# Attention, a feed-forward layer and a soft mixture of experts in one kernel: logits of the last token block taken four neuron groups at a time, its slot chain in column halves, the third block split earlier

## The chip, the core and the metric

The kernel runs on one core of one Trainium2 chip. The metric is the device time in microseconds (us) of one execution; a lower time is better. Engines are named as the profile names them: PE (TensorE), PEld (its weight loads), DVE (VectorE), ACT (ScalarE), POOL (GpSimd), SP (SyncE, which here issues every DMA).

## The reference, cut to what matters

Three stages follow each other. The constants are 4 batches, 8 heads, 576 positions, 2304 tokens, width 512, 2048 hidden neurons, 8 experts with 4 slots each (32 slots), 1024 expert neurons.

```python
def _moe_ref(x, w_in, w_out):                 # after block-causal attention; x is [2304, 512]
    h = x @ w_in                              # [2304, 2048]
    g = np.where(h >= 1, h, np.where(h <= -1, 0.0, (h + 1) ** 2 / 4))
    return (g @ w_out).astype(np.float32)

def _moe2_ref(x, phi, w1, w2):
    logits = x @ phi                          # [2304, 32]
    d = softmax over tokens (axis 0) of logits
    slot_input = (d.T @ x).reshape(8, 4, 512)
    for e in range(8):
        h = np.maximum(slot_input[e] @ w1[e], 0.0)      # w1[e] is [512, 1024]
        slot_out[e] = h @ w2[e]                         # w2[e] is [1024, 512]
    c = softmax over slots (axis 1) of logits
    return c @ slot_out                       # [2304, 512]
```

## The kernel before, in words

**Attention** (lines 46 to 345) fills the first 202 us. It leaves x transposed in SBUF: for token blocks 0 and 1 already split into a high and a low float32r part (`xt`), for blocks 2, 3 and 4 as float32 (`xw`).

**The main loop** is in `run` (L868). `BLK` (L322) has five token blocks: four of 512 tokens, the last (block 4) of 256. `UNITS` lists 69 units (b, f): token block b times one of 16 groups f of 128 hidden neurons. `h_unit` (L537) computes one unit with 12 matmuls `h`: four slices of the width times three products of high and low parts (L535). `act_unit` then makes the neurons' values `g` on ACT, POOL and DVE. Units 0 to 20 treat blocks 0 and 1 alternately and need the weight tiles `w7` to `w15`, which are still being made: a raw double `raw` is loaded, ACT scales it (`w_mul`, L457), DVE takes bits apart (`w_bits`, L463 to L466), ACT casts (L254), POOL subtracts and adds (`w_parts`, L481, L482). From unit 18 on the same is done for 16 tiles of `w_out`, where POOL adds (L474), SP stores the sum to DRAM, and PE transposes it (`wo_turn`, L495) and multiplies it by phi (`wo_phi`, L504, `wo_back`, L513) into `w2p`, which is w_out times phi. So the logits of a block are g times `w2p`.

`split(2)` (L402) takes block 2 apart: ACT casts 128x1024 values to the high part `xh` (L408), POOL subtracts to get the low part `xl` (L409), for each of two halves `u`. It stands at units 18 and 19, three units ahead of the block's first unit.

Side steps hang on unit numbers in `plan_sides` (L813): `put(k, step)` runs a step after unit k, on every engine's queue in that order. For a block they are, for each quarter q of the neuron groups and each pair u of 128-token tiles: `half` (L580; PE transposes g into `gn`, L592, ACT copies it out), with the fourth-group logits at the last u (`logits`, L599: matmuls `lt` with 32 output rows, at row 0, 32, 64 or 96 of one PSUM bank, L604); then `soft` (softmax over tokens with a running maximum), `disp` (transposes the exponentials, `et`), `slots` (L637: exponentials times `gn`, matmuls `s`, L642; DVE adds them to the running sums S, L650), and `weigh` (softmax over slots). In block 4 each of the four output places of `lt` takes the same 256 tokens (L603), so the four places hold equal copies. After block 3 `maximum`, `weights` and `total` fold the four places of S into the one tile `T`.

**The chain** (L913): `last` (the last transposes and the last four groups' logits), `soft4`, `disp4`, `slots4` (L751), two `turn` (transposes, L765), `inputs` (L768: matmuls `si` with w_out tiles `wo`, L775, which give the slots' inputs), `spread` (L779: `t_i`, and copies into `st`). **The tail** (L986) multiplies by the experts' weights: `w1` (matmuls `eh`, L998), transposes `et` of the hidden values `hN`, `w2` (matmuls `acc`, L1025), then the outputs (L1044 to L1084). The combine weights are transposed by `comb` (L973) from `n4`, made by `comb_parts` (L961): twice in the chain, three times in the tail.

**The experts' weights** come in 72 pieces `ew`: 32 of w1 (512 KB each), 24 of the first 340 columns of w2 (`in_w2a_dram`), 16 of the other 172 (`in_w2b_dram`). They go into the slots of two SBUF pools with 27 and 22 slots, which g, gn, x, w and the rest use as well. `feed` (L929) runs after each unit from 30 on and after each step of the chain and the tail; it issues up to four pieces if `room` (L351), which looks ahead on a recorded plan of slot use, leaves `spare` = 3 slots free (0 from the chain on). SP issues strictly in this order, and each DMA waits until its slot's last reader is done and until the DMA eight before it has landed.

Of the kernel before, what the change touches and what calls it, by code (L numbers as in the profile page):

```python
# [11 lines left out]
ALU = mybir.AluOpType  # L12
# [304 lines left out]
class Moe:  # L317
# [5 lines left out]
    ASIDE = 2  # L323
    CAP = {"b4": 27, "c4": 22}
# [30 lines left out]
    def room(self, key):  # L355
# [143 lines left out]
    def wo_phi(self, c):  # L499
# [7 lines left out]
        wp = self.wp = e.sp.tile([P, P], F32, tag="wp", bufs=1, name=f"wp{c}")  # L507
# [72 lines left out]
    def half(self, b, q, u):  # L580
# [5 lines left out]
        if u == 0 and q == 0 and b != 1:  # L586
            self.lt[b] = e.ppv.tile([P, 512], F32, tag="pv", name=f"lt{b}")
# [5 lines left out]
        if u == n // 256 - 1:  # L593
            self.logits(b, fs)
# [4 lines left out]
    def logits(self, b, fs):  # L599
        nc, lt = self.nc, self.lt[b]  # L600
        for f in fs:
            for j in range(4):
                o, n = (0, 256) if b == 4 else (j * P, P)  # L603
                nc.tensor.matmul(lt[32 * j:32 * j + 32, 0:n], self.e.w2p[:, f], self.gt(b, f)[:, o:o + n],  # L604
                                 start=(f == 0), stop=(f == 15))


    def soft(self, b):
# [3 lines left out]
        v["lts"] = sp.tile([P, P], F32, tag="lts", bufs=1, name=f"lts{b}")  # L612
        E = v["E"] = sp.tile([P, P], F32, tag="E", bufs=1, name=f"E{b}")
# [16 lines left out]
    def disp(self, b):  # L630
# [3 lines left out]
        v["en"] = e.sp.tile([P, P], F32, tag="en", bufs=1, name=f"en{b}")  # L634
# [17 lines left out]
    def weigh(self, b):  # L652
# [6 lines left out]
        else:  # L659
            for j in range(2):  # L660
                nc.tensor.transpose(ps[:, 32 * j:32 * j + 32], self.EL[0:32, 1, j * P:(j + 1) * P], e.ident[0:32, 0:32])
# [14 lines left out]
    def maximum(self):  # L676
# [5 lines left out]
        row = self.row = sp.tile([1, 4, 32], F32, tag="row", bufs=1, name="row")  # L682
# [28 lines left out]
    def last(self):  # L711
# [8 lines left out]
        self.logits(4, range(12, 16))  # L720
# [4 lines left out]
    def soft4(self):  # L725
        e, nc, sp = self.e, self.nc, self.e.sp
        lt = self.lt[4][:, 0:256]
        EL = self.EL
# [4 lines left out]
        nc.scalar.activation(EL[0:32, 0], lt[0:32], AF.Exp, bias=nm[0:32], accum_out=l[0:32])  # L733
# [482 lines left out]
```

## Time and profile before

| | us |
|---|---|
| median of three runs (lowest to highest) | 530.07 (528.93 to 530.76) |
| the profiled execution, its run time | 532.08 |
| its span in the profile | 530.2 |
| PE busy | 506.9 (96%) |
| PEld, DVE, ACT, POOL busy | 386.1, 335.5, 324.4, 202.0 |
| DMA | 91.01 MB, mean 172 GB/s |

The run time is the span and 1.9 us around it. The profile says for each engine when it was busy, for idle time what ended it, and for the whole program a chain of work followed back from the last instruction. Busy shares are averages over stages that have different limits; the stages here are attention (to 202), the main loop (to 466), the chain (to 479) and the tail.

### The profile page before, as it was taken

What the parts mean: (1) busy time and instruction counts of PE and PEld (TensorE: products, weight loads), DVE (VectorE), ACT (ScalarE), POOL (GpSimd) and SP (SyncE); (2) the same over time, 40 slices, a digit from 0 to 9 for tenths busy, and PEclk for the clock granted to TensorE, in tenths of its full rate; (3) what the DMA queues carried; (4) which work ended last, traced back from release to release, by engine and by line L of the source; (5) the groups of instructions that cost most, each with busy time, mean ns of one, the idle gap of its engine ahead of it and who ended that gap; (6) DMA issues with size and microseconds to landing.
All of it is one profiled execution on the core that took longest, in us unless ns stands there. A gap on an engine that the chain in (4) does not pass through costs nothing.

```text
span 530.2 us, 11838 instructions
## 1 busy us (share of the span) xinstructions
PE 506.9 (96%) x4538; PEld 386.1 (73%) x4538; DVE 335.5 (63%) x678; ACT 324.4 (61%) x732; POOL 202.0 (38%) x259
## 2 busy tenths in 40 slices
PE   6899999999999999999899999899999999989994
PEld 5688887888878787877677887788658888643463
DVE  6769988888887746888987646723554442521242
ACT  4879998888877634767868878633335444321131
POOL 3888997776777312554733214400001000000000
PEclk8779999999999999999999999999999999999998
DMA  6235435343311147113147773512266495899997
GB/s 200 91 81 163 126 84 150 90 122 101 85 53 28 51 138 285 43 40 99 56 167 230 284 268 110 178 42 80 96 255 215 131 405 172 312 329 383 410 413 297
DMA packets 42711, 91.01 MB, mean 172 GB/s; under 512 B 8736, under 2 KB 18080, under 8 KB 42656
## 3 DMA queue, kind: packets, MB, share of 16 engines
q1 hardware_dynamic: 42656, 90.26, 50.1%
q8 instruction: 36, 0.59, 0.5%
q14 instruction: 19, 0.16, 0.1%
HBM read 74.51 MB, written 14.68 MB: 168 GB/s over the span
## 4 chain that ended last, share of the span: by engine, by line
PE 82%; DVE 5%; DMA 4%; ACT 4%; issue 2%; POOL 1%; SPq 0%; ACTq 0%; DVEq 0%; POOLq 0%
PE h L535 32%; PE sc L120 7%; PE gn L592 5%; PE om L189 5%; PE lt L604 4%; PE s L642 3%; PE eh L998 3%; PE sc L113 3%; PE ps_1p L171 3%; PE ps_2p L171 2%; PE ps_3p L171 2%; PE ps_0p L171 2%; PE acc L1025 2%; PE om L194 2%; DVE wab L464 1%
## 5 line engine op out<-in xcount | busy, mean ns | idle before, releaser
L535 PE MATMUL h<-xh,w 128*128 128x512 f32 (+1 forms) x384 | 115.6, 369 | 0.0
L535 PE MATMUL h<-xt,w 128*128 128x512 f32 x384 | 99.4, 403 | 0.0
L163 POOL TENSOR_SCALAR pr<-pr,sm 128x512 f32<-128x512 f32 (+2 forms) x144 | 88.5, 632 | 25.3 <-DVE sm L158 23.6
L151 ACT ACTIVATE pr<-sc,nm 128x512 f32<-128x512 f32 (+2 forms) x144 | 78.2, 551 | 10.1 <-DVE nm L146 8.3
L569 DVE SCALAR_TENSOR_TENSOR g<-g 128x512 f32<-128x512 f32 (+1 forms) x52 | 36.9, 710 | 66.9 <-ACT g L556 66.3
L535 PEld LDWEIGHTS h<-xh,w 128*128 128x128 f32 x384 | 69.1, 189 | 13.7 <-issue 3.8
L535 PEld LDWEIGHTS h<-xt,w 128*128 128x128 f32 x384 | 68.3, 188 | 14.1 <-POOL w L482 1.8
L535 PE MATMUL h<-xl,w 128*128 128x512 f32 (+1 forms) x192 | 68.2, 355 | 0.3 <-POOL xl L409 0.3
L146 DVE TENSOR_REDUCE nm<-sc 128x2 f32<-128x1024 f32 (+1 forms) x64 | 52.3, 819 | 21.5 <-PE sc L126 21.1
L570 DVE TENSOR_TENSOR g<-h,g 128x512 f32<-128x512 f32 (+1 forms) x80 | 50.8, 636 | 15.7 <-ACT g L561 13.7
L556 ACT ACTIVATE g<-h,half 128x512 f32<-128x512 f32 (+1 forms) x52 | 32.3, 622 | 44.5 <-PE h L535 43.1
L673 POOL TENSOR_TENSOR cn<-cn,cm 128x128 f32<-128x128 f32 (+1 forms) x5 | 1.9, 379 | 140.7 <-DVE cm L672 140.7
L120 PE MATMUL sc<-K,Q 64*128 64x512 f32 (+3 forms) x384 | 47.6, 363 | 3.7 <-ACT pr L151 2.6
L254 ACT COPY gn<-gn 128x1024 f32<-128x1024 f32 x35 | 35.3, 1009 | 16.0 <-PE gn L592 15.9
L120 PEld LDWEIGHTS sc<-K,Q 64*128 64x128 f32 x384 | 30.2, 196 | 14.0 <-issue 6.1
L535 PEld LDWEIGHTS h<-xl,w 128*128 128x128 f32 x192 | 36.4, 189 | 4.5 <-POOL xl L409 0.7
L474 POOL TENSOR_TENSOR wab<-wab 128x512 f32<-128x512 f32 x16 | 22.0, 1374 | 40.4 <-DVE wab L466 20.5
L481 POOL TENSOR_TENSOR wab<-wab,w 128x256 f32<-128x256 f32 (+1 forms) x23 | 22.6, 982 | 37.5 <-ACT w L254 20.3
L592 PE MATMUL gn<-ident,g 128*128 128x128 f32 x280 | 36.5, 273 | 0.1
L592 PEld LDWEIGHTS gn<-ident,g 128*128 128x128 f32 x280 | 31.9, 140 | 5.2 <-issue 2.5
L464 DVE SCALAR_TENSOR_TENSOR wab<-wab 128x512 uint32<-128x512 uint32 (+1 forms) x39 | 28.5, 731 | 10.3 <-ACT wab L457 7.0
L558 ACT ACTIVATE g<-h,half 128x512 f32<-128x512 f32 x28 | 19.2, 686 | 22.2 <-PE h L535 20.0
(222 smaller groups left out, 898.1 us busy)
## 6 DMA issues: line engine op xcount, KB each, us to landing
ew<-in_w_dram SPq DMA_DIRECT2D x32, 512.0 KB, 5.6
raw<-in_w_in_dram SPq DMA_DIRECT2D x16, 512.0 KB, 5.8
raw<-in_w_out_dram SPq DMA_DIRECT2D x16, 512.0 KB, 4.2
ew<-in_w2a_dram SPq DMA_DIRECT2D x16, 510.0 KB, 9.1
ew<-in_w2b_dram SPq DMA_DIRECT2D x16, 344.0 KB, 6.7
kn<-in_k_dram SPq DMA_DIRECT2D x16, 288.0 KB, 3.2
qn<-in_q_dram SPq DMA_DIRECT2D x16, 288.0 KB, 4.4
vn<-in_v_dram SPq DMA_DIRECT2D x16, 256.0 KB, 3.4
```

The lines of the kernel that those rows point to most:

```text
L120: nc.tensor.matmul(sc[:, h, 0:n], self.Q[r, qa, 128 * i:128 * i + 128], self.K[r, ka, 0:n], start=(k == 0), stop=False)
L146: nc.vector.tensor_reduce(out=self.negm[:, 2 * i:2 * i + 2], in_=self.scs[i][:, :, 0:128 * (i + 1)], axis=AX.X, op=ALU.max, negate=True)
L151: self.nc.scalar.activation(pr, sc, AF.Exp, bias=self.negm[:, b:b + 1], accum_out=self.acc[:, b, 0:1])
L163: self.nc.gpsimd.tensor_scalar(out=pr, in0=pr, scalar1=self.sums[:, b:b + 1], scalar2=1.0, op0=ALU.mult, op1=ALU.mult)
L171: nc.tensor.transpose(ps[:, u * P:(u + 1) * P], self.pr[b][:, kc * P:(kc + 1) * P], e.ident)
L254: nc.scalar.copy(dst, src)
L464: v.scalar_tensor_tensor(out=Au, in0=Au, scalar=3, in1=Bu, op0=ALU.logical_shift_left, op1=ALU.bitwise_or)
L535: nc.tensor.matmul(ph[:, 0:n], w[:, wi, kk], self.x(b, kk, xi)[:, 0:n], start=(kk + m == 0), stop=(kk + m == 5))
L556: nc.scalar.activation(g, ph, AF.Relu, bias=e.half[:, 0:1], scale=0.5)
L569: nc.vector.scalar_tensor_tensor(out=g, in0=g, scalar=1.0, in1=g, op0=ALU.min, op1=ALU.mult)
L570: nc.vector.tensor_tensor(out=g, in0=ph, in1=g, op=ALU.max)
L592: nc.tensor.transpose(ps[:, j, i * P:(i + 1) * P], self.gt(b, f)[:, o:o + P], e.ident)
```

## The change

**Logits of block 4.** For groups f below `SPLIT` = 14 one matmul takes place of four: group f goes to output place f % 4 alone, in columns 256 to 511 of the bank, so that the four places hold partial sums of different groups. `gather` (after the third `half`) does groups 12 and 13 and lets ACT copy the partial sums to `part`; `collect` adds the four places with one 128x256 matmul by `sel4` into columns 0 to 255. Groups 14 and 15 are added there as before, by four matmuls each.

**Order.** Block 3's logits are all computed right after block 2's `soft`, in two batches of eight groups, and no longer between block 3's transposes; `soft`, `disp`, `slots`, `maximum`, `weights`, `weigh` and `total` of blocks 2 and 3 move up, block 3's first `slots` by five units. `split(2)` is called before unit 0 and at unit 1 in place of units 18 and 19. The POOL subtraction of every `split` is done in two halves of 128x512.

**Chain.** `slots4`, `inputs` and `spread` are done by column halves u = 0, 1, each with a PSUM tile of its own, and `spread(1)` stands inside the first `w1` group. `comb` for blocks 2 and 3 moves from the tail into the chain, and `comb` works on 64 columns where it had the same 64 twice (ACT copies the result twice).

**Slots.** The tiles `EL`, `E`, `en`, `lts` and `wp` become parts of one fixed tile `y`, which frees one slot from unit 65 on. `room` leaves 3 slots free up to unit 57, then 1. SP's order of DMAs is the same in both kernels.

```diff
+    SPLIT = 14
...
-            if base + len(gone) - k > self.cap - (self.spare if t < self.bend else 0):
+            if base + len(gone) - k > self.cap - (3 if t < self.middle else 1 if t < self.bend else 0):
...
-                self.nc.gpsimd.tensor_tensor(out=lo, in0=self.xw[i, u], in1=hi.bitcast(F32), op=ALU.subtract)
+                for a in range(0, 1024 // n, 512 // n):
+                    c = slice(a, a + 512 // n)
+                    self.nc.gpsimd.tensor_tensor(out=lo[:, c], in0=self.xw[i, u][:, c], in1=hi[:, c].bitcast(F32), op=ALU.subtract)
...
     def logits(self, b, fs):
...
+            if b == 4 and f < self.SPLIT:
+                j = f % 4
+                nc.tensor.matmul(lt[32 * j:32 * j + 32, 256:512], self.e.w2p[:, f], self.gt(b, f),
+                                 start=(f < 4), stop=(f + 4 >= self.SPLIT))
+                continue
             for j in range(4):
                 o, n = (0, 256) if b == 4 else (j * P, P)
...
+    def gather(self):
+        self.logits(4, range(12, self.SPLIT))
+        self.part = self.e.sp.tile([P, 256], F32, tag="part", bufs=1, name="part")
+        self.nc.scalar.copy(self.part, self.lt[4][:, 256:512])
+
+    def collect(self):
+        self.nc.tensor.matmul(self.lt[4][:, 0:256], self.e.sel4, self.part, start=True, stop=False)
...
-        self.logits(4, range(12, 16))
+        self.collect()
+        self.logits(4, range(self.SPLIT, 16))
...
+    def slots4(self, u):
+        e, nc = self.e, self.nc
+        ps, o = e.psc.tile([P, 2, 512], F32, tag="sc", name=f"s4{u}")[:, 0, 0:256], slice(256 * u, 256 * u + 256)
         for j in range(2):
             for c in range(4):
-                nc.tensor.matmul(ps[32 * c:32 * c + 32], self.EL[:, 2, 32 * j:32 * j + 32], self.gn[4, c, 0][:, j],
+                nc.tensor.matmul(ps[32 * c:32 * c + 32], self.last_en[:, 32 * j:32 * j + 32], self.gn[4, c, 0][:, j, o],
                                  start=(j == 0), stop=(j == 1))
...
+        for u in range(2):
+            ps, o = self.si[u], slice(256 * u, 256 * u + 256)
+            for t in (2 * r, 2 * r + 1):
...
+            if r == 1:
+                e.copy("A", self.T[:, o], ps)
...
+            if b == 2:
+                put(free, "soft", 2)
+                for i, step in enumerate((("disp", 2), ("weigh", 2), ("logits", 3, range(8)))):
+                    put(free + 1, *step)
+                for i, step in enumerate((("slots", 2, 0), ("logits", 3, range(8, 16)), ("soft", 3))):
+                    put(free + 2, *step)
+                put(free + 3, "slots", 2, 1)
+                put(free + 4, "disp", 3)
+                put(free + 6, "maximum")
+                put(free + 7, "weights")
+                put(free + 8, "weigh", 3)
+        put(at_half[3, 1] + 2, "slots", 3, 0)
+        put(free + 1, "slots", 3, 1)
+        put(free + 2, "total")
...
+        self.w_mul(READY)
+        self.w_bits(READY)
+        parts = list(self.split(2))
+        parts[0]()
         for k, (b, f) in enumerate(units):
...
+            if k == 1:
+                parts[1]()
...
-        steps = (self.soft4, lambda: self.comb(0), self.disp4, lambda: self.comb(1), self.slots4, self.clear,
-                 lambda: self.turn(0), lambda: self.turn(1), lambda: self.inputs(0), lambda: self.inputs(1), self.spread)
+        steps = ((self.soft4,), (self.comb, 0), (self.comb, 1), (self.disp4,), (self.slots4, 0),
+                 (self.slots4, 1), (self.clear,), (self.turn, 0), (self.comb, 2), (self.turn, 1), (self.inputs, 0),
+                 (self.inputs, 1), (self.spread, 0), (self.comb, 3), (self.drop, "n4"))
...
-        w1(0)
+        w1(0, lambda: self.spread(1))
```

How the order moves, at three places. First POOL where the main loop begins: `pr` is attention's last work there, `wab` and `w` are `w_parts` of the weight tiles 7 and 8. Before:

```order
L163 TENSOR_SCALAR pr_184<-pr_184,sm_3_2763 128x128
L481 TENSOR_TENSOR wab_3046<-wab_3046,w_3070 128x512
L482 TENSOR_TENSOR w_3070<-wab_3046 128x512
L481 TENSOR_TENSOR wab_3090<-wab_3090,w_3119 128x512
L482 TENSOR_TENSOR w_3119<-wab_3090 128x512
```

Now:

```order
L163 TENSOR_SCALAR pr_184<-pr_184,sm_3_2763 128x128
L412 TENSOR_TENSOR xl_3054<-xw_148,xh_3053 128x512 x2
L484 TENSOR_TENSOR wab_3047<-wab_3047,w_3076 128x512
L485 TENSOR_TENSOR w_3076<-wab_3047 128x512
L412 TENSOR_TENSOR xl_3081<-xw_149,xh_3080 128x512 x2
L484 TENSOR_TENSOR wab_3101<-wab_3101,w_3130 128x512
L485 TENSOR_TENSOR w_3130<-wab_3101 128x512
```

Two halves of `xl` stand ahead of tile 7's pair, and two ahead of tile 8's.

Second PE at the last logits, in `last` and the chain's first steps; `gn` are the transposes, `ct` is `comb`, `et` is `disp4`. Before:

```order
L716 MATMUL gn_5670<-ident,g_12_5477 128x128 x6
L604 MATMUL lt_5434<-g_12_5477,w2p 32x256 x16
L716 MATMUL gn_5670<-ident,g_12_5477 128x128 x2
L973 MATMUL ct_5708<-identr,n_5526 128x128 x4
L743 MATMUL et_5715<-ident,EL 128x32 x2
L973 MATMUL ct_5719<-identr,n_5526 128x128 x4
```

Now:

```order
L733 MATMUL gn_5633<-ident,g_12_5516 128x128 x6
L622 MATMUL lt_5488<-part,sel_124 128x256
L613 MATMUL lt_5488<-g_12_5516,w2p 32x256 x8
L733 MATMUL gn_5633<-ident,g_12_5516 128x128 x2
L1004 MATMUL ct_5660<-identr,n_5565 64x128 x4
L1004 MATMUL ct_5668<-identr,n_5565 64x128 x4
L760 MATMUL et_5675<-ident,y 128x32 x2
```

Sixteen narrow matmuls became eight and one wide one, and both `ct` stand ahead of `et`.

Third PE at block 3's first `slots` (matmuls `s`). Before, they stand between units h_12 and h_13 of block 4, ahead of `t_m` (`maximum`):

```order
L642 MATMUL s_5481<-gn_5087,en_5432 32x512 x2
L642 MATMUL s_5481<-gn_5143,en_5432 32x512 x2
L642 MATMUL s_5481<-gn_5190,en_5432 32x512 x2
L642 MATMUL s_5481<-gn_5251,en_5432 32x512 x2
L681 MATMUL t_m<-ident,nm 1x128
```

Now, between h_7 and h_8:

```order
L593 MATMUL gn_5313<-ident,g_8_4575 128x128 x2
L593 MATMUL gn_5313<-ident,g_10_4645 128x128 x2
L658 MATMUL s_5324<-gn_5122,y 32x512 x2
L658 MATMUL s_5324<-gn_5202,y 32x512 x2
L658 MATMUL s_5324<-gn_5249,y 32x512 x2
L658 MATMUL s_5324<-gn_5287,y 32x512 x2
L538 MATMUL h_8_5342<-xh_4835,w_3130 128x256
```

The four `gn` tiles that `s` reads last become free for pieces `ew` five units sooner.

## Rows read from the trace of the kernel before

**Rows 1.** The page: busy time, share of the span and instructions

```profile
PE 506.9 (96%) x4538; PEld 386.1 (73%) x4538; DVE 335.5 (63%) x678; ACT 324.4 (61%) x732; POOL 202.0 (38%) x259
```

**Rows 2.** The chain of waits in order of time: start, us, what, pieces

```profile
202.28 52.94 PE h L535 x228
...
434.99 1.44 PE h L535 x12
...
446.75 1.86 PE lt L604 x32
448.62 1.63 PE h L535 x12
...
466.76 1.91 PE lt L604 x32
470.79 1.95 PE s L751 x16
474.20 3.71 PE si L775 x32
...
507.40 0.85 PE t_o L1044 x2
510.52 6.77 DMA ew<-in_w2b_dram
```

**Rows 3.** PE's waits: line waited for, us in total, times, longest

```profile
PE aside L495 <- POOL wab L474: 3.0, 4, 1.9
...
PE aside L495 <- ACT wp L508: 1.0, 1, 1.0
...
PE et L743 <- ACT EL L733: 0.7, 1, 0.7
PE t_s L765 <- DVE T L756: 0.7, 1, 0.7
PE acc L1025 <- DMA ew<-in_w2b_dram: 0.6, 2, 0.4
PE t_i L788 <- ACT T L254: 0.5, 1, 0.5
PE h L535 <- POOL xl L409: 0.3, 1, 0.3
```

**Rows 4.** Stretches: PE, PEld, DVE, ACT, POOL busy; PEclk; DMA share; GB/s

```profile
440.00:451.00 11.00, 11.00 (x133) 8.87 (x135) 3.69 (x12) 5.71 (x11) 0.00 (x0) 1.00 0.50 169
...
476.00:511.00 35.00, 34.08 (x366) 14.73 (x362) 8.64 (x28) 6.83 (x19) 0.29 (x1) 1.00 1.02 401
511.00:525.00 14.00, 11.07 (x149) 8.33 (x141) 5.73 (x11) 5.23 (x14) 0.00 (x0) 1.00 1.03 405
```

**Rows 5.** SP's waits from 466 to 530, the same columns

```profile
SPq L947 <- DMA ew<-in_w2a_dram: 15.3, 19, 2.4
```

**Rows 6.** SP's timeline at 476

```profile
476.14 0.33 SPq L947 DMA_DIRECT2D ew<-in_w2a_dram  x1
```

**Rows 7.** POOL's timeline, 204 to 218: start, us, instruction, idle before

```profile
209.34 1.62 POOL L482 TENSOR_TENSOR w<-wab 128x512 fp32r<-128x512 f32 x1
213.41 1.29 POOL L481 TENSOR_TENSOR wab<-wab,w 128x512 f32<-128x512 f32 x1 [2.45 <-ACT w L254]
214.78 1.62 POOL L482 TENSOR_TENSOR w<-wab 128x512 fp32r<-128x512 f32 x1
```

**Rows 8.** DVE's timeline, 206 to 214

```profile
208.72 1.10 DVE L569 SCALAR_TENSOR_TENSOR g<-g 128x512 f32<-128x512 f32 x1 [0.61 <-ACT g L556]
...
211.35 0.69 DVE L464 SCALAR_TENSOR_TENSOR wab<-wab 128x512 uint32<-128x512 uint32 x1
```

**Rows 9.** DVE's timeline, 257 to 264

```profile
258.89 2.50 DVE L464 SCALAR_TENSOR_TENSOR wab<-wab 128x512 uint32<-128x512 uint32 x1 [0.44 <-ACT wab L457]
```

**Rows 10.** POOL's timeline, 257 to 266

```profile
258.44 2.41 POOL L409 TENSOR_TENSOR xl<-xw,xh 128x1024 fp32r<-128x1024 f32 x1 [3.19 <-ACT xh L408]
```

**Rows 11.** ACT's timeline, 256 to 259

```profile
257.26 1.03 ACT L408 CAST xh<-xw 128x1024 fp32r<-128x1024 f32 x1
```

More of the change, by code (lines that the diff above doesn't have):

```diff
@@ L770, in inputs @@
         if r == 0:
-            self.si = e.psc.tile([P, 2, 512], F32, tag="sc", name="si")[:, 0]
-        for t in (2 * r, 2 * r + 1):
-            for c in range(4):
-                f = 4 * c + t
-                nc.tensor.matmul(self.si[32 * c:32 * c + 32], self.sg[:, t, 32 * c:32 * c + 32], self.wo[f // 2][:, f % 2],
-                                 start=(t == 0), stop=(t == 3))
+            self.si = [e.psc.tile([P, 2, 512], F32, tag="sc", name=f"si{u}")[:, 0, 0:256] for u in range(2)]
@@ L777, in inputs, with spread @@
+        for u in range(2):
+            ps, o = self.si[u], slice(256 * u, 256 * u + 256)
+            for t in (2 * r, 2 * r + 1):
+                for c in range(4):
+                    f = 4 * c + t
+                    nc.tensor.matmul(ps[32 * c:32 * c + 32], self.sg[:, t, 32 * c:32 * c + 32], self.wo[f // 2][:, f % 2, o],
+                                     start=(t == 0), stop=(t == 3))
+            if r == 1:
+                e.copy("A", self.T[:, o], ps)
         self.drop(*[f"wo{2 * c + r}" for c in range(4)])
-    def spread(self):
+    def spread(self, u):
@@ L780, in spread @@
         e, nc = self.e, self.nc
-        s4 = self.T
-        for k0 in (0, 2):
-            c = slice(k0 * P, k0 * P + 256)
-            e.copy("AD"[k0 // 2], s4[:, c], self.si[:, c])
-        for k0 in (0, 2):
-            ps = e.ptr.tile([P, 2, 32], F32, tag="tr", name=f"t_i{k0}")
-            for k in range(2):
-                nc.tensor.matmul(ps[:, k], s4[:, (k0 + k) * P:(k0 + k + 1) * P], e.sel4[:, 0:32], start=True, stop=True)
-            own = self.st[:, 0:924].rearrange("p (e r) -> p e r", r=132)[:, :, 32 * k0:32 * k0 + 64]
-            nc.vector.tensor_copy(own.rearrange("p e (k s) -> p e k s", s=32)[:, :, :, 0:4],
-                                  ps[:, :, 0:28].rearrange("p k (e i) -> p e k i", i=4))
-            own = self.st[:, 896 + 32 * k0:960 + 32 * k0].rearrange("p (k s) -> p k s", s=32)
-            nc.vector.tensor_copy(own[:, :, 28:32], ps[:, :, 28:32])
@@ L794, in spread @@
-        self.drop("T")
+        k0 = 2 * u
+        ps = e.ptr.tile([P, 2, 32], F32, tag="tr", name=f"t_i{k0}")
+        for k in range(2):
+            nc.tensor.matmul(ps[:, k], self.T[:, (k0 + k) * P:(k0 + k + 1) * P], e.sel4[:, 0:32], start=True, stop=True)
+        own = self.st[:, 0:924].rearrange("p (e r) -> p e r", r=132)[:, :, 32 * k0:32 * k0 + 64]
+        nc.vector.tensor_copy(own.rearrange("p e (k s) -> p e k s", s=32)[:, :, :, 0:4],
+                              ps[:, :, 0:28].rearrange("p k (e i) -> p e k i", i=4))
@@ L899, in run @@
                 (getattr(self, fn) if isinstance(fn, str) else fn)(*a)
[L900 to L904 removed]
+            if k == 66:
+                self.n4 = self.new([P, 4, 256], F32R, "n4")
+                for i in range(4):
+                    self.comb_parts(i)
+            if k == 57:
+                self.middle, self.spare = len(self.tape), 1
             if k > 29:
@@ L978, in comb @@
         self.cT[blk] = self.ct[:, nth % 2]
-        nc.scalar.copy(self.cT[blk][:, 0:nj * P], ps[:, 0:nj * P])
+        for a in (0, 64):
+            nc.scalar.copy(self.cT[blk][a:a + 64, 0:nj * P], ps[0:64, 0:nj * P])
     def fill(self, ps, n):
@@ L1101, in tail @@
         w2(0, 1)
-        comb(order[2])
-        comb_parts(order[3])
+        comb_parts(4)
         w2(0, 2)
@@ L1108, in tail @@
         fold(0)
-        comb(order[3])
-        comb_parts(order[4])
         w2(1, 0, (1,))
@@ L1114, in tail @@
             if g == 0:
-                comb(order[4])
+                comb(4)
             w2(1, 1 + g)
```

98 lines of the change are left out of this document (43 added, 55 removed).

## The prediction, made before the changed kernel was run

> **What bounds the kernel now.** I read the page first: PE is busy 506.9 us of the span [rows 1], so PE is the engine to shorten, if nothing else sets the end. The chain of waits in order of time [rows 2] runs through PE from 202.28, where the main loop begins, to the tail; what PE itself waits for [rows 3] adds only a few us. But PE alone is not the whole bound at the end. In the stretches [rows 4] the DMA engines run at a share of 1.02 and 401 GB/s from 476 to 511, and 405 GB/s to 525, while in 440 to 451 they stand at 0.50. The last item of the chain is a piece of `in_w2b_dram` that lands at 510.52+6.77 = 517.29 [rows 2]. SP's waits say the same from the other side: after 466, nineteen pieces of w2 waited for the landing of an earlier piece, 15.3 us together [rows 5]. The first of the saturated issues starts at 476.14 [rows 6], when the first half of `si` has given back four `wo` slots. From there to the end of the span are 530.2-476.1 = 54.1 us, and I take this **restart** as the point that sets the end: 54.1 us of weights and outputs follow it, the number of pieces loaded ahead of it is the same in both kernels, and SP's order is the same. PE is only just slower than the stream: it waited 0.6 us for `in_w2b_dram` [rows 3]. So the change is worth what it brings the restart forward.
>
> **Early split.** Taking `split(2)` out of units 18 and 19 removes the port trouble there. With `xl` on POOL for 2.41 us [rows 10], a DVE line that takes 0.69 at 211.35 [rows 8] takes 2.50 at 258.89 [rows 9]; the `w_out` sums arrive late, and PE waits 3.0 for `wab`, 1.0 for `wp`, 0.3 for `xl` [rows 3]. I take all 4.3 (bounds 0, if other work takes the place, and 4.3). It costs something at the loop's start. Four halves of `xl`, each about 2.41/2 = 1.2, join POOL ahead of tile 8's pair. Before, tile 8's low part was ready at 214.78+1.62 = 216.40 [rows 7]. PE asks for it at matmul 62 of the loop; one takes 52.94/228 = 0.2322 [rows 2], so at 202.28+62x0.2322 = 216.68: a margin of 0.28. After, the cast `xh` (1.03 on ACT [rows 11]) delays the `g` line of DVE (1.10 at 208.72 [rows 8]) into POOL's L482, which ends at 209.34+1.62 = 210.96 [rows 7]; then half of an `xl` (1.2) and a DVE line alternate, and L464 ends at 214.8 where it ended at 212.04. Tile 8 is 2.75 late, less the margin about **2.5 us of wait**. Bounds: 0 (POOL fits its halves between) and four halves, 4.8; I take 2.5, since it follows from the rows of this very place. Front in all: -4.3+2.5 = **-1.8**.
>
> What the row at 258.89 shows is a lock and not a slowdown: DVE's line stood for as long as POOL's transfer ran [rows 9, 10]. The Trainium skill, page "SBUF — State Buffer", section "Who interferes with whom", says that DVE and GpSimd share a port pair under an exclusive lock, that a DVE operation with two SBUF inputs and a GpSimd one reading SBUF keep each other out entirely, and that "Issue order, not op shape, decides who blocks." The trace agrees with 2.50 beside 0.69. By that rule nothing is gained from halving, and all four halves could fall on DVE's time, so that the sum would be 2.3 us higher.
>
> **Logits of block 4.** Before, three calls of 16 matmuls take 1.86 each [rows 2] (one row of the three stands there), the last 1.91. Four matmuls at the four output places evidently run beside each other: 16 in 1.86 is 0.465 for four. With one matmul per group, a call of four groups is 0.465, so three calls save 4.2 less what `gather` does: calls of groups 0 to 11 become 3x0.465, `gather` adds 0.465 at most. `collect` is one 128x256 matmul; nearest row: two of 128x340 take 0.85 for `t_o` [rows 2], so 0.425 each, and I take 0.5 with its start. The last two groups take 0.93. New: 1.4+0.465+0.5+0.93 = 3.3 for 3x1.86+1.91 = 7.5, **-4.2**. Bounds: the four places must take different moving data now; the slot matmuls of block 4 do so already, two rounds of 512 columns in 1.95 [rows 2], that is 0.49 for 256 columns, so 3.4 at most. Without any overlap a group costs 0.465, see rival 4. ACT's copy `part` lies under the transposes of groups 12 to 14.
>
> **Order.** A unit's matmuls after `lt` take 1.63, after transposes 1.44 [rows 2], 0.19 more for a change of kind. Block 3's four batches of logits leave the transposes, and two batches stand among other steps: 4x0.19 = **-0.7** (bounds -0.8 and 0). Last logit: 466.76+1.91 = 468.67 before, 463.7 after these two, the front aside.
>
> Block 3's `slots`, five units earlier, and w1's pieces that wait for them: DMA is at 0.50 in 440 to 451 [rows 4], so earlier slots fill a hole and nothing waits there on PE. Counted 0. If they did not come earlier, the stream would still have that slack. `room` with 1 spare slot in place of 3 does the same: 0.
>
> **Chain.** Halves let DVE or ACT work on one half while PE works on the other. That removes the wait of `t_s` for T (0.7) and of `t_i` (0.5) [rows 3]; the second lies behind the restart and counts for PE only. Against it `comb` of block 2 (four transposes, about 0.5 as its sister's) now stands ahead of `si`, and both earlier `comb` stand ahead of `et`, which covers the 0.7 wait for `EL` [rows 3] but exposes the copy behind `et` that the second `comb` covered. Net to the restart I take **-0.2** (bounds -0.7 and +0.6). `si` itself, 3.71 for 16 of 512 columns [rows 2], has the same columns in 32 of 256: 0.
>
> **Tail.** Two `comb` leave it and the `t_i` wait goes, so PE gets ahead by some 1.5 us more than the restart does, and gives it back in waits for `in_w2b_dram`, which become about 2 us. The restart sets the end.
>
> **Sum.** -1.8-4.2-0.7-0.2 = **-6.9**: restart 469.2, span 523.3, run time 532.08-6.9 = 525.2. The profiled execution lies 2.0 above the median of the three runs, so I set the difference against the median: 530.07-6.9 = **523.2**. Bounds of the terms together give 520.6 to 525.5 for this course.
>
> **Rivals.** About 0.3% (1.6 us) can be told from no change, so faster means below 528.5, slower above 531.7.
>
> 1. *The stream cannot restart earlier.* If its slots or landings ahead of the restart do not move with PE, only the front is gained: 530.07-1.8 = 528.3. For it: 401 GB/s, no reserve [rows 4]. Against: the stretch 440 to 451 has room, and the first saturated issue waits for `si`, not for a landing. Chance 0.10.
> 2. *No wait at the loop's start.* POOL's halves slip between DVE's lines, the whole 4.3 stays: 530.07-4.3-5.1 = 520.6. For it: POOL is idle 2.45 ahead of 213.41 [rows 7]. Against: DVE has hardly a gap there [rows 8]. Chance 0.13.
> 3. *Slower: the delay stays through the tiles.* The start's delay puts DVE's lines and POOL's into each other at every one of the nine conversions `w7` to `w15`, and each loses one POOL line of 1.29 [rows 7]: 9x1.29 = 11.6, so 530.07-4.3+11.6-5.1 = 532.3. It decides from the point where PE's waits between 210 and 258 add up to more than 4.3+5.1 = 9.4. For it: the margin is only 0.28. Against: PE consumes a tile in two units, 24x0.2322 = 5.6 us, and a conversion on POOL is 2.9. Chance 0.06.
> 4. *The narrow matmuls do not overlap.* 14x0.465+0.5+0.93 = 7.9 in place of 3.3: 527.7. Against: the row of block 4's slots. Chance 0.05.
>
> **How the numbers follow.** The forecast keeps 0.66. The range runs from 519.8, a little below rival 2, to 528.3, rival 1; outside are rival 3, half of rival 1 and the forecast's own tails, together under 0.2. Faster: 0.66+0.13+0.05, half of rival 1, less 0.03 for tails = 0.86; same: 0.08; slower: 0.06.
>
> **What would show it.** Right: waits for `wab`, `wp` and `xl` near 250 to 270 are gone, one wait of `h` on `w` of 2 to 3 us near 216; `lt` of block 4 at about 0.47 per call, `collect` at 0.5; the first `in_w2a_dram` that waits for `si` issues near 469; 54 us from there to the end; DMA share still near 1.0, PE waiting about 2 us for `in_w2b_dram`. Wrong: a restart that is early with an end that is not (the stream then has another bound), `lt` near 1.9 per call, or waits on `w` repeated every tile.

## The result and the profile of the changed kernel

| us | before | changed |
|---|---|---|
| median of four runs (lowest to highest) | 530.41 (528.93 to 532.35) | 523.70 (522.42 to 524.74) |
| run time and span of the profiled execution | 532.08, 530.2 | 523.28, 521.5 |
| PE busy | 506.9 | 500.6 |

The ratio is 0.9853, 95% interval 0.9820 to 0.9887 (the two medians alone divide to 0.9873): the change makes the kernel faster, by 6.7 us between the medians. The forecast was 6.9 us and a time of 523.2.

The page of the changed kernel answers to [rows 1]; PE is as full as before, of a shorter span:

```profile
PE 500.6 (96%) x4504; PEld 384.5 (74%) x4504; DVE 331.6 (64%) x672; ACT 327.0 (63%) x734; POOL 203.9 (39%) x264
```

Its chain of waits (start, us, what) answers to [rows 2]. L608 are the narrow logits (here groups 8 to 13), L622 is `collect`, L613 the last two groups; the restart is the SP line below it, from SP's timeline (start, us, instruction), which answers to [rows 6]:

```profile
456.35 0.99 PE lt L608 x12
...
459.63 0.43 PE lt L622 x2
460.06 1.08 PE lt L613 x16
...
463.11 2.06 PE s L768 x32
...
466.23 3.59 PE si L793 x64
```

```profile
468.11 0.80 SPq L980 DMA_DIRECT2D ew<-in_w2a_dram  x2
```

The reader sees the last logit end at 460.06+1.08 = 461.1 (468.7 before) and the restart at 468.1 (476.1 before). The two narrow calls ahead of these, groups 0 to 3 and 4 to 7, stand in the chain of the stretch from 446 to 470:

```profile
447.58 0.57 PE lt L608 x8
...
451.84 0.57 PE lt L608 x8
```

What PE waits for (total, times, longest) answers to [rows 3]:

```profile
PE h L538 <- POOL w L485: 1.4, 1, 1.4
PE aside L498 <- ACT w2p L517: 1.4, 1, 1.4
...
PE aside L498 <- ACT y L511: 1.0, 1, 1.0
...
PE acc L1058 <- DMA ew<-in_w2b_dram: 0.6, 2, 0.4
PE et L760 <- ACT y L750: 0.5, 1, 0.5
...
PE s L768 <- DVE row L761: 0.3, 1, 0.3
...
PE t_s L781 <- DVE T L772: 0.2, 1, 0.2
```

The 3.0 for `wab` and the 0.3 for `xl` are gone, the 1.0 behind `wp` (now in `y`) stayed; one wait for `w` is new. The 1.4 for `w2p` is not: the kernel before has it too.

```profile
PE aside L495 <- ACT w2p L514: 1.5, 1, 1.5
```

And the stretches (columns as in [rows 4]):

```profile
440.00:451.00 11.00, 11.00 (x97) 7.87 (x96) 5.75 (x16) 4.84 (x9) 0.40 (x1) 1.00 1.02 407
470.00:505.00 35.00, 34.40 (x392) 15.66 (x391) 8.75 (x24) 7.83 (x18) 0.29 (x1) 1.00 1.03 403
```

The hole of 440 to 451 is filled with pieces of w1 (share 1.02 where it was 0.50), and the stream after the restart runs at the same rate as before. From the restart to the end, the kernel before moved 20.35 MB and the changed one 19.90 (two views, in this order):

```profile
DMA packets 6998, 20.35 MB, mean 376 GB/s; under 512 B 784, under 2 KB 912, under 8 KB 6994
```

```profile
DMA packets 6847, 19.90 MB, mean 373 GB/s; under 512 B 768, under 2 KB 896, under 8 KB 6842
```

In both, 36 pieces were issued ahead of the restart, so less of them was still under way in the changed kernel. At 403 GB/s the 0.45 MB are 1.1 us.

**Where the time went, by stages.** Units of the main loop are counted from 0; the start of a unit is the start of its first `h` in PE's timeline, 12 matmuls for each. In the two profiled executions:

| stage, us | before | changed | difference | forecast |
|---|---|---|---|---|
| to the loop's start | 202.2 | 200.4 | -1.8 | 0 |
| unit 0 to unit 25 (front) | 75.4 | 74.4 | -1.0 | -1.8 |
| unit 25 to unit 56 | 138.9 | 138.9 | 0.0 | 0 |
| unit 56 to the last logit | 52.1 | 47.4 | -4.7 | -4.9 |
| last logit to the restart | 7.5 | 7.0 | -0.5 | -0.2 |
| restart to the end | 54.0 | 53.4 | -0.7 | 0 |

The first line is no part of the change. It arises at 30 to 34 us in attention, where the program is the same: PE's granted clock (the number after the five engines) came back to its upper level earlier in one execution than in the other. The two rows are of the kernel before and of the changed one:

```profile
30.00:34.00 4.00, 4.00 (x21) 4.00 (x22) 2.89 (x6) 2.88 (x7) 1.88 (x6) 0.56 0.32 90
```

```profile
30.00:34.00 4.00, 4.00 (x38) 3.66 (x39) 3.72 (x9) 3.46 (x9) 2.65 (x7) 1.00 0.32 92
```

Over the profiles of all kernels here the loop began between 200.3 and 203.5. That is about as much as the runs of one kernel differ (528.93 to 532.35 for the kernel before), and it is why the experiments below are read by stages first.

**The loop's start.** POOL's timeline answers to [rows 7]; L412 is `xl`, L484 and L485 make a tile of w:

```profile
202.28 3.25 POOL L412 TENSOR_TENSOR xl<-xw,xh 128x512 fp32r<-128x512 f32 x2 [12.12 <-ACT xh L409]
206.19 1.29 POOL L484 TENSOR_TENSOR wab<-wab,w 128x512 f32<-128x512 f32 x1 [0.65 <-ACT w L254]
207.56 1.29 POOL L485 TENSOR_TENSOR w<-wab 128x512 fp32r<-128x512 f32 x1
208.81 3.18 POOL L412 TENSOR_TENSOR xl<-xw,xh 128x512 fp32r<-128x512 f32 x2
213.26 1.60 POOL L484 TENSOR_TENSOR wab<-wab,w 128x512 f32<-128x512 f32 x1 [1.28 <-ACT w L254]
214.94 1.60 POOL L485 TENSOR_TENSOR w<-wab 128x512 fp32r<-128x512 f32 x1
```

and DVE's answers to [rows 8]; L467 is the line that was L464:

```profile
207.68 1.72 DVE L572 SCALAR_TENSOR_TENSOR g<-g 128x512 f32<-128x512 f32 x1 [1.36 <-ACT g L559]
...
210.94 1.59 DVE L467 SCALAR_TENSOR_TENSOR wab<-wab 128x512 uint32<-128x512 uint32 x1
```

Tile 8's low part is ready at 214.94+1.60 = 216.54, 16.1 after the loop's start; before it was 14.2. PE stood still for 1.43. Then came what no term of the forecast held: the clock fell behind this wait.

```profile
216.00:220.00 4.00, 3.40 (x10) 2.77 (x11) 3.24 (x6) 1.08 (x2) 2.14 (x2) 0.70 0.04 12
220.00:224.00 4.00, 4.00 (x17) 3.20 (x16) 2.70 (x5) 1.73 (x3) 1.28 (x1) 0.87 0.39 125
```

From unit 3 to unit 8 it took 17.3 us against 14.0 before: 3.3 lost, 1.7 of it by the wait and 1.6 by the slower clock, as the experiments show. From unit 20 to 25 it took 15.5 against 19.9: 4.4 gained, where 4.3 were forecast.

### The profile page after: what moved, and what is told of

It reads as the page before. It is cut to its first block, busy times and chain, and to the rows that moved or that the text cites. A ratio compares the mean times of both kernels' runs of the same rounds, so it can differ in the third digit from the quotient of the medians.

```text
span 521.5 us, 11780 instructions
## 1 busy us (share of the span) xinstructions
PE 500.6 (96%) x4504; PEld 384.5 (74%) x4504; DVE 331.6 (64%) x672; ACT 327.0 (63%) x734; POOL 203.9 (39%) x264
## 4 chain that ended last, share of the span: by engine, by line
PE 81%; ACT 4%; DMA 3%; DVE 3%; issue 1%; POOL 1%; SPq 0%; ACTq 0%; DVEq 0%; POOLq 0%
PE h L538 33%; PE sc L120 7%; PE gn L593 5%; PE om L189 5%; PE s L658 3%; PE eh L1031 3%; PE ps_1p L171 2%; PE sc L113 2%; PE lt L613 2%; PE ps_2p L171 2%; PE ps_3p L171 2%; PE acc L1058 2%; PE om L194 2%; PE ps_0p L171 2%; DMA ew<-in_w2b_dram 1%
## 5 line engine op out<-in xcount | busy, mean ns | idle before, releaser
L538 PE MATMUL h<-xt,w 128*128 128x512 f32 x384 | 101.2, 408 | 1.6 <-POOL w L485 1.4
L538 PEld LDWEIGHTS h<-xt,w 128*128 128x128 f32 x384 | 69.5, 191 | 16.2 <-POOL w L485 2.7
L484 POOL TENSOR_TENSOR wab<-wab,w 128x256 f32<-128x256 f32 (+1 forms) x23 | 23.2, 1010 | 22.5 <-ACT w L254 21.3
L467 DVE SCALAR_TENSOR_TENSOR wab<-wab 128x512 uint32<-128x512 uint32 (+1 forms) x39 | 25.4, 651 | 10.0 <-ACT wab L460 6.6
L561 ACT ACTIVATE g<-h,half 128x512 f32<-128x512 f32 x28 | 19.3, 689 | 19.9 <-PE h L538 15.8
```

Source lines behind the costliest of these rows:

```text
L538: nc.tensor.matmul(ph[:, 0:n], w[:, wi, kk], self.x(b, kk, xi)[:, 0:n], start=(kk + m == 0), stop=(kk + m == 5))
```

## The experiments

Each ran beside the kernel before on the same chip; ratios are to it. The chips differ: the kernel before had a median of 531.37 beside `split_late` to `old_order`, of 532.96 beside `split_mid` to `half_w2b` and of 530.28 beside the last three, so medians of different groups are compared by their ratios, each of which is uncertain by some 0.3% (1.6 us). The stages come from each kernel's profile; "3 to 8" and "0 to 25" are units.

| kernel | median us | ratio (interval) | 3 to 8 | 0 to 25 | 56 to restart | restart to end |
|---|---|---|---|---|---|---|
| before | 530.41 | 1 | 14.0 | 75.4 | 59.6 | 54.0 |
| changed | 523.70 | 0.9853 (0.9820 to 0.9887) | 17.3 | 74.4 | 54.4 | 53.4 |
| split_late | 525.56 | 0.9883 (0.9852 to 0.9913) | 14.0 | 75.0 | 54.4 | 54.5 |
| split_ahead | 522.95 | 0.9846 (0.9816 to 0.9876) | 15.6 | 72.6 | 54.4 | 53.4 |
| four | 527.48 | 0.9914 (0.9885 to 0.9943) | 15.7 | 72.8 | 58.3 | 52.5 |
| old_order | 525.01 | 0.9871 (0.9842 to 0.9900) | 15.7 | 72.8 | 55.2 | 53.9 |
| split_mid | 525.29 | 0.9872 (0.9842 to 0.9902) | 14.0 | 75.6 | 54.4 | 55.4 |
| whole_xl | 524.26 | 0.9849 (0.9814 to 0.9884) | 16.0 | 73.1 | 54.4 | 52.9 |
| fill | 523.07 | 0.9824 (0.9795 to 0.9853) | 15.7 | 72.9 | 54.4 | 53.5 |
| half_w2b | 521.59 | 0.9806 (0.9768 to 0.9845) | 17.3 | 74.4 | 54.4 | 51.8 |
| again | 523.76 | 0.9871 (0.9830 to 0.9913) | 15.7 | 72.8 | 54.4 | 52.8 |
| spread2 | 522.80 | 0.9848 (0.9806 to 0.9890) | 15.1 | 72.5 | 54.4 | 54.2 |
| spread4 | 522.38 | 0.9841 (0.9805 to 0.9878) | 14.5 | 71.6 | 54.4 | 53.1 |

### split_late: the split back at units 18 and 19

```diff
-        parts = list(self.split(2))
-        parts[0]()
...
-            if k == 1:
-                parts[1]()
...
-                if b == 2:
-                    continue
-                put(2, "x_out", b, u)
-                put(pos(b, 0) - 6, "x_in", b, u)
+                if b > 2:
+                    put(2, "x_out", b, u)
+                    put(pos(b, 0) - 6, "x_in", b, u)
                 put(pos(b, 0) - 3 + u, fn)
```

> The changed kernel with split(2) back at units 18 and 19; the halves of xl stay. Theory (the early split buys 4.35 us between units 20 and 24 and pays 3.3 us at units 4 to 6): PE's wait for tile 8 at the loop's start is gone, the waits for wab, wp and xl of 3 to 4.3 us are back, the time is 1.05 us above the changed kernel, about 524.8 us. Rival A (what was paid at the start has nothing to do with the split): the full 4.35 is lost, about 528. Rival B (the waits near 260 came from the long xl instruction, and halves cure them in any place): both go, about 520.4.

PE's waits in this kernel:

```profile
PE aside L498 <- POOL wab L477: 3.1, 2, 2.2
...
PE aside L498 <- ACT y L511: 1.2, 1, 1.2
...
PE h L538 <- POOL xl L412: 0.2, 1, 0.2
```

Of the waits of [rows 3], those for `wab` and `xl` are back at 3.3 together, though `xl` still comes in halves, so rival B falls; the 1.2 behind `y` had never gone. Unit 3 to 8 takes 14.0 again, so what is lost there in the changed kernel is the price of the early split, and rival A falls. The front is 0.6 us longer than the changed kernel's in its profile and 2.2 longer than in the executions without the fall of the clock. By the ratios the time is 1.6 us above the changed kernel's, where 1.05 was expected.

### split_ahead: both parts ahead of tile 7's scaling

```diff
+        for part in self.split(2):
+            part()
         self.w_mul(READY)
         self.w_bits(READY)
-        parts = list(self.split(2))
-        parts[0]()
...
-            if k == 1:
-                parts[1]()
```

> The changed kernel with both parts of split(2) put ahead of tile 7's scaling, where ACT stands idle for 2.3 us and POOL for 12 us at the end of attention. Theory (tile 8 is late only because xl stands between tile 7's and tile 8's POOL lines): PE's wait of 1.4 us and the fall of its clock to 0.70 in 216 to 220 both go, 3.3 us less, about 520.4 us. Rival (DVE and POOL get in each other's way wherever four more POOL lines are put): w7 or w8 is late again by one or two lines, 522 to 525.

POOL's timeline of this kernel:

```profile
203.17 5.69 POOL L412 TENSOR_TENSOR xl<-xw,xh 128x512 fp32r<-128x512 f32 x4 [11.54 <-ACT xh L409]
208.82 1.75 POOL L484 TENSOR_TENSOR wab<-wab,w 128x512 f32<-128x512 f32 x1
210.64 1.60 POOL L485 TENSOR_TENSOR w<-wab 128x512 fp32r<-128x512 f32 x1
```

The idle time at attention's end could not be used: ACT's cast `xh` waited for attention's last matmuls `om` and began only at 202.0. (The likely reason is that `xh` takes a slot which these matmuls still read.) So tile 7 was late instead of tile 8, with a wait of 1.4 and no fall of the clock. Of the theory's gain of 3.3 the front shows 1.8, and nearly all of it is the fall that did not come: against `again` below, the changed kernel without the fall, the front is 0.2 shorter. The place gained next to nothing, and the rival was right that one tile is late.

### four: every group of block 4 by four matmuls

```diff
-    SPLIT = 14
+    SPLIT = 0
...
-        put(k, "gather")
...
-        self.collect()
-        self.logits(4, range(self.SPLIT, 16))
+        self.logits(4, range(12, 16))
```

> The changed kernel with SPLIT at 0: each group of block 4 by four matmuls as before, no gather and no collect. Theory (the term of 4.2 us): three calls of 1.86 and one of 1.91 are back, the restart of the weights is 4.2 us later, the time is 4.2 above the changed kernel, about 527.9 us. Rival (the weights' stream, not PE, sets the restart and the end): 523.7 to 525.

The chain of waits of this kernel (the rows of `lt` alone):

```profile
449.58 1.86 PE lt L613 x32
...
455.13 1.86 PE lt L613 x32
...
460.93 1.86 PE lt L613 x32
...
465.08 1.91 PE lt L613 x32
```

The three calls of 1.86 and the one of 1.91 are back, and the restart lies 58.26-54.41 = 3.85 later behind unit 56 (4.2 expected). The rival fell: the weights' stream followed. By the ratios the time is 0.61% or 3.2 us above the changed kernel's.

### old_order: block 3's steps where they were

In `plan_sides` the side steps of blocks 2 and 3 stand again as in the kernel before, `half` calls `logits` for block 3 too, and `comb_parts(3)` comes one unit later.

> The changed kernel with block 3's logits, soft, slots, maximum, weights and total in the old order. Theory: four changes between lt and h are back, 0.7 us, and pieces of w1 come later, so that more of them are still under way at the restart and the stretch from there to the end is 54.1 us again instead of 53.4: together 1.4 us, about 525.1 us. Rival 1 (earlier slots are worth nothing): 0.7 us, 524.4. Rival 2 (the early slots are what lets the restart move at all): 4 us or more, above 527.5.

The restart is 55.2-54.4 = 0.8 later, as the four changes between `lt` and `h` ask for. The pieces of w1 do come later; the stretch

```profile
440.00:451.00 11.00, 11.00 (x121) 7.91 (x120) 5.27 (x15) 4.91 (x10) 0.00 (x0) 1.00 0.58 195
```

has its hole again. But the 53.9 from the restart to the end are inside the scatter of this stretch, 52.5 to 55.4 over the kernels that move the same bytes. So rival 1 is not contradicted: the early slots are worth nothing that can be seen, and the 0.7 us that the changed profile gained there is not shown to be theirs. The time does not decide between the theory's 1.4 us and the rival's 0.7: by the ratios it is 1.0 above the changed kernel's. Rival 2 fell.

### split_mid: the split after units 16 and 17

```diff
+                if b == 2:
+                    put(16 + u, fn)
+                    continue
```

(and without the two early calls.)

> The changed kernel with the two parts of split(2) after units 16 and 17, behind nearly all tiles of w and two units ahead of the place they had in the kernel before. Theory (xl does harm only where a tile or a w_out sum has under 1.2 us to spare): no wait at the loop's start, and xl ends some 5 us before the first w_out sum is needed, so that the waits of 3 to 4.3 us near 260 shrink to 0 to 1.5: unit 25 begins 1 to 3 us earlier against the loop's start than in the changed kernel, the time is 521 to 522.7. Rival 1 (the tiles of w have no time to spare anywhere): a wait of 1 to 2.5 us for tile 15 takes the place of that for tile 8, 523 to 524. Rival 2 (two units are too few): the waits near 260 stay at 3 or more, 523.5 to 525.

```profile
PE h L538 <- POOL w L485: 2.8, 1, 2.8
```

PE's wait moved to tile 15 and doubled; between units 20 and 25 another 1.4 us was lost. The front took 75.6, no less than before the change. Rival 1 was right about the place, with a wait longer than its 1 to 2.5: tile 15 has no time to spare either, as tile 7 (`split_ahead`) and tile 8. The stretch from the restart, 55.4, was the longest of all (see the last section).

The clock did not fall behind this wait, which ended at 256.42:

```profile
252.00:256.00 4.00, 1.61 (x8) 0.99 (x6) 3.40 (x4) 1.38 (x2) 3.92 (x4) 1.00 0.17 68
256.00:260.00 4.00, 3.58 (x16) 2.93 (x17) 3.93 (x4) 2.51 (x4) 3.50 (x3) 1.00 0.00 0
```

### whole_xl: each xl by one POOL line

```diff
-                for a in range(0, 1024 // n, 512 // n):
-                    c = slice(a, a + 512 // n)
-                    self.nc.gpsimd.tensor_tensor(out=lo[:, c], in0=self.xw[i, u][:, c], in1=hi[:, c].bitcast(F32), op=ALU.subtract)
+                self.nc.gpsimd.tensor_tensor(out=lo, in0=self.xw[i, u], in1=hi.bitcast(F32), op=ALU.subtract)
```

> The changed kernel with each xl made by one POOL line of 128x1024, not by two halves. Theory (POOL and DVE shut each other out line by line, so the sum of POOL's lines counts and not their length): the wait for tile 8 stays at 1 to 2 us, the time within 1 us of the changed kernel. Rival (a long line holds DVE for its whole length and DVE's chain for the tile loses 1.2 us more): a wait of 2.5 us or more, 1.2 us above.

The wait for tile 8 is 1.4 in this profile too, unit 0 to 25 takes 73.1 against 72.8 in `again`. The halves are worth 0.3 us at most; the sum of POOL's lines counts.

### fill: PE works through the wait

```diff
+        if (b, f, kk) == (0, 8, 0):
+            for _ in range(7):
+                nc.tensor.matmul(ph[:, 0:n], w[:, 0, kk], self.x(b, kk, 0)[:, 0:n], start=True, stop=True)
```

> The changed kernel with seven more matmuls (1.6 us, overwritten at once) on PE ahead of the one that waits for tile 8, so that PE works through the wait. Theory (the clock fell to 0.5 for 4 us in the profile of the changed kernel because PE had stood still for 1.4 us, and it falls in some executions only): the clock of 216 to 224 is 1.00, the wait is gone, and the time is that of an execution without the fall, 0 to 1.5 us below the changed kernel's median; its profile shows unit 8 at +1.8 to +2.0 from the changed kernel's unit 3, against +3.3 there. Rival (the clock falls there for another reason): it falls again, and the time is the same or 0.2 above.

```profile
216.00:220.00 4.00, 4.00 (x18) 3.10 (x18) 3.79 (x6) 2.34 (x4) 2.10 (x3) 1.00 0.03 6
220.00:224.00 4.00, 4.00 (x20) 3.30 (x19) 3.37 (x6) 1.98 (x4) 3.00 (x2) 1.00 0.38 131
```

The wait and the fall are gone, and unit 3 to 8 takes 15.7 (the seven matmuls taken out of the count of units), as in the profiles with the wait and without the fall. This is as the theory has it, but it is one profile, and others without the fill show the clock at 1.00 too (next). So the cause of the fall is not shown, and the run times do not settle how often it comes.

### half_w2b: half the bytes of the last weights

```diff
-                nc.sync.dma_start(t, e.w2[key[3]][ex, :, q[0]:q[-1] + 1])
+                if key[3] == 1:
+                    t = t[:, 0:2]
+                nc.sync.dma_start(t, e.w2[key[3]][ex, :, q[0]:q[0] + 2] if key[3] else e.w2[0][ex, :, q[0]:q[-1] + 1])
...
-                                         self.weight(2, 2 * pr + i, fs, d)[:, a], start=(k == 0), stop=(k == 15))
+                                         self.weight(2, 2 * pr + i, fs, d)[:, a % 2 if d else a], start=(k == 0), stop=(k == 15))
```

> The changed kernel, in which each of the 16 pieces of in_w2b_dram brings half of its rows and the matmuls use these twice: the other half of these weights is left out. About 2.8 MB less, 7.0 us at 403 GB/s, with the same work on PE. Theory (the stream sets the end, with PE close behind it): the end comes 0.6 to 1.5 us earlier, and PE no longer waits for in_w2b_dram; the rest of the 7 us is hidden by PE. Rival 1 (PE is far ahead of the stream): 3 us or more. Rival 2 (PE alone sets the end): within 0.3.

From the restart to the end it took 51.8, which is 1.6 less than the changed kernel's 53.4 and 0.7 less than the shortest of the twelve profiles with all bytes (52.5 to 55.4). PE's waits name `in_w2b_dram` no more, and from 490 on the chain of waits has no DMA, where a piece of `in_w2b_dram` stands in that of all twelve. So the stream sets the end in the twelve, with PE not far behind it: 7 us less of transfers gained 0.7 to 1.6 us here. Rival 1 is not borne out; against rival 2 there are 0.7 us and one profile. By the ratios the time is 2.5 us below the changed kernel's, with intervals that overlap.

### again, spread2, spread4: the second xl in pieces behind the tiles

The first is the changed kernel itself. In the others the second `xl` is cut into 2 or 4 pieces, and one piece follows the pair of tile 8, 9 and so on (the edit shown is that of `spread4`).

```diff
             if k == 1:
-                parts[1]()
+                hi, lo = self.xt[2, 1] = [self.new([P, 2, 512], F32R, f"x{c}21") for c in "hl"]
+                self.nc.scalar.copy(hi, self.xw[2, 1])
+            if k in (3, 5, 7, 9):
+                hi, lo = self.xt[2, 1]
+                c = slice((k - 3) // 2 * 256, (k - 3) // 2 * 256 + 256)
+                flat = lambda t: t.rearrange("p a n -> p (a n)")[:, c]
+                self.nc.gpsimd.tensor_tensor(out=flat(lo), in0=flat(self.xw[2, 1]), in1=flat(hi).bitcast(F32), op=ALU.subtract)
+                if k == 9:
+                    self.drop("xw21")
```

> The changed kernel itself, beside the two that follow: 522.5 to 525 us. Theory (the fall of the clock behind the wait for tile 8 comes in some executions only): the wait of 1.4 us for tile 8 is there again, and the clock in 216 to 224 is either about 0.7 or 1.00.

> The changed kernel, in which the second xl's two POOL halves stand behind the pairs of tile 8 and tile 9 (one each) and not together ahead of tile 8's pair. Theory (a tile is late by what stands ahead of it beyond its margin of some 0.3 us): the wait for tile 8 goes, tiles 9 and 10 are late by one half less POOL's idle time, together 0 to 0.6 us: from the loop's start to unit 20 it takes 1.2 to 1.8 us less than in the changed kernel without its fall of clock, and the time is 521.5 to 523. Rival (DVE is as tight as POOL, so each half costs its own 1.2 us wherever it stands): waits of about 1 us at tiles 9 and 10, no gain.

> The same with four quarters of 128x256 behind the pairs of tiles 8 to 11. Theory: no tile is late, 1.8 us less than the changed kernel without the fall, 521.5 to 522.5. Rival: each quarter costs 0.5 us or more, the time is that of the changed kernel.

In `again` the wait of 1.4 is there, and the clock did not fall:

```profile
216.00:220.00 4.00, 2.43 (x10) 1.43 (x9) 3.86 (x6) 3.04 (x5) 3.13 (x2) 1.00 0.01 2
```

Of the six profiles that have the wait for tile 8 (changed, again, four, old_order, whole_xl, half_w2b), two show the fall. With four pieces PE's one wait for a tile is

```profile
PE h L538 <- POOL w L485: 0.6, 1, 0.6
```

and unit 0 to 25 takes 71.6, 1.2 less than in `again`; with two pieces there are three waits of 1.1 together, and it takes 72.5. With four pieces the theory was somewhat too good (no wait and 1.8 us were expected; to unit 20 it takes 56.0 against 57.3 in `again`), and the rival fell. With two the theory failed: to unit 20 it takes 57.0, 0.3 less than in `again` where 1.2 to 1.8 were expected. The waits for tiles 8, 9 and 10 are 0.6, 0.3 and 0.3, so the rival's waits of 1 us did not come either, but its "no gain" is nearer. The median of `spread4` is 1.4 below that of `again` on the same chip, and its ratio of 0.9841 (0.9805 to 0.9878) makes it faster than the kernel before. Against the changed kernel the gain is seen in the stages; the intervals of the two overlap.

## Why the prediction was right

**The bound.** That the end hangs on the restart held: in the changed kernel it came 8.0 us earlier and the end 8.7 (1.8 of either from before the main loop), and in `four` it went 3.85 us back and the time 3.2. What was too simple is the fixed 54.1: the kernel before moved 0.45 MB more after its restart, and the changed kernel and its variants took 52.5 to 55.4 for the same 19.9 MB. The piece that lands at 517.29 is the last DMA of the chain in [rows 2] and not its last item; 12.9 us follow it.

**The bounds.** 520.6 to 525.5 is not what the bounds of the terms give together. All low ones give -4.3-4.2-0.8-0.7, or 520.1; 525.5 is the forecast with the bound of 4.8 us alone, and all high ones give 531.4.

**Early split, gain.** 4.3 forecast, 4.4 measured between units 20 and 25; `split_late` undoes it. The mechanism was right for `wab` and `xl`, but one part was booked wrongly: the 1.0 for `wp` lies behind unit 25 and stayed (0.7 to 1.3 in the profiles). So the 4.4 are 1.1 more than the waits for `wab` and `xl` in PE's rows. Between units 20 and 25 of the kernel before PE has 16.67 busy and 3.2 idle, of the changed kernel 15.60 and none, with the same 78 matmuls: the missing 1.1 stands as busy time. The weight loads show longer waits there (line waited for, total, times, longest, of the kernel before), so part of a wait probably counts as busy in PE's rows:

```profile
PEld aside L495 <- POOL wab L474: 4.7, 4, 2.3
...
PEld h L535 <- POOL xl L409: 0.7, 1, 0.7
```

**Early split, price.** 2.5 forecast. Its place (tile 8) and its cause (POOL's and DVE's lines by turns, the tile 1.9 late with 0.28 to spare) were right; the wait costs 1.7 where the clock holds. The mis-sized term is the lateness, 2.75 forecast and 16.1-14.2 = 1.9 measured. What was missing is the second price, 1.6 us of PE at the lower clock behind the wait, in two of six profiles. Front in all: -1.8 forecast, -1.0 with the fall and -2.6 (`again`) without it.

The rule of the Trainium skill that I set beside this term (page "SBUF — State Buffer", section "Who interferes with whom") agrees with the trace on both sides of the lock: DVE's L467 took 1.59 while the two met, 0.69 alone, POOL's halves took 1.6 each where the long line of [rows 10] makes 1.2, and halving bought 0.3 at most. My estimate by it, all four halves on the tile's time and the sum 2.3 higher, is not what the trace shows: the tile was 1.9 late, not 4.8.

**Logits.** -4.2 forecast; -3.85 by `four`, and the rows give the same: 0.57+0.57+0.99+0.43+1.08 = 3.64 in place of 3x1.86+1.91 = 7.49. Narrow matmuls at the four output places do run beside each other with different data: six took 0.99, where one matmul of as many columns, `collect`, took 0.43. The terms that were too small are the calls of four groups, 0.57 for 0.465 each, and the last two groups, 1.08 for 0.93.

**Order.** -0.7 forecast, -0.8 by `old_order`. That earlier slots for w1 are worth nothing is not contradicted: the hole in the DMA came back and the end did not move beyond the scatter.

**Chain.** -0.2 forecast, -0.5 measured from the last logit to the restart (7.5 and 7.0). The wait of `t_s` fell from 0.7 to 0.2 and one of 0.3 ahead of `s` is new; no run took the term apart.

**Tail: the step that failed.** "PE gets ahead by some 1.5 us more than the restart does, and gives it back in waits for `in_w2b_dram`, which become about 2 us." They stayed at 0.6. From the first `si` to the first `t_o` PE saved 0.8 (474.20 to 507.40 before, 466.16 to 498.60 now), about what the stream gained in the same profile, so the two kept step. Over the other profiles the wait goes with the stream's own time and not with PE's lead: none is listed in `four` (52.5 from the restart to the end), 0.4 in `again` (52.8), 1.0 in `old_order` (53.9), 1.9 in `split_mid` (55.4). The sum did not hang on this step.

**The rivals.** Rival 1 fell with the restart at 468.1, rival 4 with the rows of `lt`. Rival 2 is half true: without the fall the front gains 2.6 of 4.3. Rival 3 fell: after tile 8 no wait follows, units 8 to 20 take 33.3 us in both kernels. `split_mid` shows how near it was: the same four POOL lines cost 2.8 at tile 15. That the forecast of 523.2 was met within 0.5 is partly luck, since errors cancel: the front is better than forecast where the clock holds and worse where it falls, the logits give 0.35 less, and the chain 0.3 and the stream 0.7 more.

## What to carry to other kernels

Work moved off a crowded stretch lands on another; count each line that it puts ahead of a tile that is just in time, and compare the sum with that tile's margin, which may be 0.3 us. If the tiles are in time by so little all along, cut the moved work into pieces smaller than the idle time of a round and give one to each (`spread4`), rather than look for one better place (`split_ahead`, `split_mid`). When an engine and a DMA stream end together, shorten what both wait for, here the restart; taking 7 us from the stream alone gave 0.7 to 1.6.

## What the runs showed of the hardware that was not expected

A wait of PE of 1.4 us can cost twice its length: behind the same wait at the same matmul the granted clock fell in two of six profiles (0.70 in 216 to 220 and 0.87 in 220 to 224 in the changed kernel's, which is some 3.4 us at the lower level of 1.2 GHz), and stayed at 1.00 in four. It stayed there too behind the wait of 2.8 us in `split_mid`, so the length of the wait alone does not decide it. In the two, the loop had begun at 200.4 and 200.7, in the four at 201.3 to 203.5; whether that is the reason was not tried. The stage before, attention, differs by up to 3.3 us between executions, and the difference goes with the moment at which the clock came back to 2.4 GHz: in the thirteen profiles it came back for the last time there between 29.6 and 35.2 us, the loop began at 200.3 to 200.7 in the three with 29.6 to 30.1, and at 202.8 to 203.5 in the four with 34.2 or later.

The same 19.9 MB of weights and outputs took between 52.5 and 55.4 us from the restart to the end, with the same order of DMAs. The traces show where the difference arises: in the 8 us that begin 2 us after the restart. There the stream ran at 402 GB/s in `again` (52.8) and at 349 in `split_late` (54.5), with PE, ACT and DVE equally busy, and in the 16 us after it at 410 and 411:

```profile
471.09:479.09 8.00, 7.87 (x75) 2.76 (x74) 0.99 (x7) 1.93 (x4) 0.00 (x0) 1.00 1.02 402
479.09:495.09 16.00, 16.00 (x168) 6.46 (x168) 4.04 (x11) 2.29 (x5) 0.29 (x1) 1.00 1.03 410
```

```profile
472.36:480.36 8.00, 7.87 (x75) 2.76 (x74) 0.99 (x7) 1.94 (x4) 0.00 (x0) 1.00 1.01 349
480.36:496.36 16.00, 16.00 (x168) 6.46 (x168) 4.05 (x11) 2.29 (x5) 0.29 (x1) 1.00 1.03 411
```

Over the eleven profiles with these bytes the rate in that stretch was 344 to 402, the three slowest (344, 344, 349) belong to the three longest times (54.2 to 55.4), and the two fastest (400, 402) to the two shortest. `split_mid` lost more later (395 in 494.66 to 510.66, 411 or 412 in the others). Why the rate differs, at a DMA share of 1.00 to 1.02, was not tried.
